# Loading the value windows of a banded attention: own rows of all blocks, and border rows apart

## Chip, core and metric

The kernel runs on one core of one Trainium2 chip. The metric is the device time of one execution in microseconds (us). Three runs of the kernel before took 838.1, 845.5 and 845.78 us; their median is 845.5 us.

## What is computed

An attention with two branches over q, k and v of shape 8 batches x 8 heads x 576 tokens x 64 (float32), and behind it a mixture of 8 experts over the 4608 rows of 512 numbers that the attention gives. The change lies in the local branch of the attention:

```python
pos = np.arange(S)
mask = np.abs(pos[:, None] - pos[None, :]) < 4
scores = np.where(mask, scale * q @ k.T, -1e9)
out_local = softmax(scores) @ v
out_d = softmax(scale * q_d @ k_d.T) @ v_d      # q, k, v averaged over groups of 4 tokens
out = np.repeat(out_d, 4, axis=2) + out_local
# then: each row goes to the expert of its highest score, relu(x @ w1[e]) @ w2[e], times its weight
```

A token sees itself and three neighbours on either side. So a block of 64 queries needs 70 rows of values: its own 64, three above and three below.

## The kernel before, in words

The attention comes first, then the experts. The 8 batches are cut in halves of four heads ("a half": 16 in all), and a half in two units of two heads (32 units). The loop of `attention` is a pipeline written out by hand: in one pass it transposes q and k of unit a (`qk_T`, L344, L345), forms the scores of unit a - 1 (`scores`, L373 and L378: L373 is one matmul in each pass, which marks the pass in the trace), pools k, q and v by four on GpSimd (`pooled`, L358; `pooled_v`, L367), builds a diagonal matrix of maxima on GpSimd (`diagonal`, L405), and for unit a - 2 transposes the weights (`weights_T`, L432), computes the pooled weights (`weights_dT`, L445 and L450: L450 needs that diagonal) and multiplies weights by values (`values_d`, L460; `values`, L478). GpSimd takes its work in order, so the diagonal waits behind the pooling of v. `rows` (L493, L498) transposes results back, `place` picks experts; between passes the first expert's weights are loaded in pieces (`st`, L797), measured (L753, L756, L761) and split.

All loads of the attention go out on SyncE's (SP's) queue, in the order of the program. Twice in a pass pair: `load_v` (L319, the pooled branch's values, tile `ld_v`, one buffer, needed by L367 one pass later), at the end of a pass `load` (L311, eight loads of q and k, 96 partitions x 6 x 64 numbers each) and `load_w` (the value windows, tile `vw`, two buffers, needed by L478 three passes later). Weight pieces and the stores of results (`xd`, L521, L522) go in between.

`vw` holds for one half nine windows of 70 rows for four heads: 70 partitions x 9 windows x 4 heads x 64 numbers. Window g starts at token 64 g - 3; the first window lacks its three upper rows and the last its three lower ones, which are zeroed once at the start. `load_w` fills it with six loads: window 0 from partition 3 on (L326, 67 partitions, four heads), the seven windows in the middle head by head (L329, 70 partitions, four loads), and the last window (L330, 67 partitions, four heads). Every contiguous run is one row of 64 numbers, 256 bytes.

Of the kernel before, what the change touches and what calls it, by code (L numbers as in the profile page):

```python
# [19 lines left out]
B, H, S, D = 8, 8, 576, 64  # L20
# [3 lines left out]
G, QB = S // 64, 32  # L24
WK, WV = QB + 6, 64 + 6
# [23 lines left out]
class Kern:  # L49
# [128 lines left out]
    def attention(self, ctx):  # L178
# [46 lines left out]
        load_v(0)  # L225
        load(1)
        load_w(0)
        load_w(1)
        tail, mid = [], []
        for i in range(-2, n + 1):  # L230
# [58 lines left out]
            if d >= 0 and d % 2 == 1:  # L289
                load_w(d // 2 + 2)  # L290
# [32 lines left out]
    def load_w(self, b, hf, vw):  # L323
        nc = self.nc
        g = self.v[b, 4 * hf:4 * hf + 4]
        nc.sync.dma_start(out=vw[3:, 0], in_=g[:, :WV - 3].rearrange("h p d -> p h d"))  # L326
        for c in range(4):
            mid = bass.AP(g.tensor, g[c, 61:62].offset, [[D, WV], [64 * D, G - 2], [1, D]])
            nc.sync.dma_start(out=vw[:, 1:G - 1, c], in_=mid)  # L329
        nc.sync.dma_start(out=vw[:WV - 3, G - 1], in_=g[:, S - WV + 3:].rearrange("h p d -> p h d"))  # L330

    def bank(self):
        return self.bk.tile([128, 512], F32, name="bank")
# [910 lines left out]
```

## Time and profile before

| | |
|---|---|
| three runs | 838.1, 845.5, 845.78 us |
| the profiled execution | 839.92 us |
| its span, from the first instruction to the last | 838.2 us |
| mean granted TensorE clock | 0.953 |
| busy: PE, DVE, ACT, POOL | 91%, 63%, 50%, 51% of the span |
| attention (first to last matmul of L478) | 24.4 to 342.8 us |

The shares are means over two stages that have different limits, so the stretches of the attention are to be read by themselves. PE is TensorE, PEld its weight loads, DVE is VectorE, ACT ScalarE, POOL GpSimd, SPq the queue on which SyncE issues DMAs. The duration of a row of SPq is the time for which the queue was held by that issue; the transfer goes on behind it. What stands in brackets behind a row is how long its engine sat idle before it and what ended that.

### The profile page before, as it was taken

What the parts mean: (1) busy time and instruction counts of PE and PEld (TensorE: products, weight loads), DVE (VectorE), ACT (ScalarE), POOL (GpSimd) and SP (SyncE); (2) the same over time, 40 slices, a digit from 0 to 9 for tenths busy, and PEclk for the clock granted to TensorE, in tenths of its full rate; (3) what the DMA queues carried; (4) which work ended last, traced back from release to release, by engine and by line L of the source; (5) the groups of instructions that cost most, each with busy time, mean ns of one, the idle gap of its engine ahead of it and who ended that gap; (6) DMA issues with size and microseconds to landing.
All of it is one profiled execution on the core that took longest, in us unless ns stands there. A gap on an engine that the chain in (4) does not pass through costs nothing. (4 is left out here: it accounts for less than half of the span.)

```text
span 838.2 us, 22778 instructions
## 1 busy us (share of the span) xinstructions
PE 761.3 (91%) x8100; PEld 464.3 (55%) x8100; DVE 524.9 (63%) x1501; ACT 417.8 (50%) x807; POOL 430.6 (51%) x815
## 2 busy tenths in 40 slices
PE   7599999999899998969989989899889998998993
PEld 5388778887788887524434444344434444443441
DVE  6358879997769999774653555556373456446430
ACT  3234554444544453326565566667566347546620
POOL 7056564765546667452764445464454535543521
PEclk8769999999889999989998999999999999999997
DMA  8567767576667676583897796969898759858651
GB/s 153 111 140 166 202 131 180 125 206 136 199 134 183 122 176 193 154 205 76 213 193 147 176 222 178 214 140 271 147 218 192 152 116 268 148 132 237 152 97 27
DMA packets 282902, 138.96 MB, mean 166 GB/s; under 512 B 249970, under 2 KB 259186, under 8 KB 282752
## 3 DMA queue, kind: packets, MB, share of 16 engines
q1 hardware_dynamic: 274944, 116.05, 62.0%
q0 software_dynamic: 6560, 19.03, 8.8%
q10 hardware_dynamic: 1248, 2.11, 0.7%
q8 instruction: 66, 1.08, 0.5%
q14 instruction: 84, 0.69, 0.3%
HBM read 213.05 MB, written 20.33 MB: 278 GB/s over the span
## 5 line engine op out<-in xcount | busy, mean ns | idle before, releaser
L1080 PE MATMUL bank<-w1h,xT 128*128 128x512 f16 x328 | 126.3, 385 | 19.1 <-DMA xT<-x 18.6
L1105 PE MATMUL bank<-w2h,hT 128*128 128x512 f16 x328 | 125.0, 381 | 9.8 <-DMA hT<-h 9.8
L1081 PE MATMUL bank<-w1l,xT 128*128 128x512 f16 x328 | 126.1, 384 | 1.6 <-DVEq L925 1.6
L1082 PE MATMUL bank<-w1h,xT 128*128 128x512 f16 x328 | 126.1, 384 | 0.0
L1107 PE MATMUL bank<-w2h,hT 128*128 128x512 f16 x328 | 125.0, 381 | 0.0
L1106 PE MATMUL bank<-w2l,hT 128*128 128x512 f16 x328 | 125.0, 381 | 0.0
L1118 POOL DMA_INDIRECT out_dram<-o,ids x41 | 46.8, 1142 | 134.6 <-ACTq L920 97.1
L1090 DVE SCALAR_TENSOR_TENSOR h<-bank,h 128x512 f16<-128x512 f32 x82 | 55.3, 689 | 93.7 <-ACT h L1089 61.7
L1089 ACT ACTIVATE h<-bank 128x512 f16<-128x512 f32 x82 | 47.7, 595 | 97.1 <-PE bank L1082 57.9
L367 POOL TENSOR_TENSOR pool_v<-ld_v 72x256 f32<-72x256 f32 x64 | 48.6, 770 | 75.7 <-DMA ld_v<-in_v_dram 74.4
L345 ACT ACTIVATE kq<-bank 128x288 f32<-128x288 f32 x128 | 44.1, 416 | 76.3 <-PE bank L344 72.9
L753 ACT ACTIVATE junk<-st 128x1024 bf16<-128x1024 f32 (+1 forms) x30 | 67.5, 2251 | 6.8 <-DVE place L673 5.6
L358 POOL TENSOR_TENSOR pool_kq<-kq 128x288 f32<-128x288 f32 x62 | 43.3, 714 | 48.7 <-ACT kq L345 48.6
L1002 POOL DMA_INDIRECT xg<-xd,ids x41 | 45.5, 1109 | 43.5 <-issue 15.3
L1080 PEld LDWEIGHTS <-xT 128*128 128x128 f16 x328 | 32.5, 99 | 60.9 <-DMA xT<-x 22.1
L1105 PEld LDWEIGHTS <-hT 128*128 128x128 f16 x328 | 34.8, 106 | 45.3 <-DMA hT<-h 10.6
L67 POOL TENSOR_SCALAR nw_t<-nw_y,nw_a 128x1 f32<-128x1 f32 x120 | 52.3, 436 | 12.1
L386 ACT ACTIVATE a<-a 128x342 f32<-128x342 f32 x32 | 15.6, 489 | 83.7 <-DVE a L385 83.7
L1032 DVE SCALAR_TENSOR_TENSOR x<-xg,sc,x 128x512 f16<-128x512 f32 x41 | 30.9, 753 | 42.1 <-ACT x L1029 42.1
L1082 PEld LDWEIGHTS <-xT 128*128 128x128 f16 x328 | 32.5, 99 | 41.7 <-issue 4.1
L1081 PEld LDWEIGHTS <-xT 128*128 128x128 f16 x328 | 32.5, 99 | 39.2 <-issue 2.9
L1107 PEld LDWEIGHTS <-hT 128*128 128x128 f16 x328 | 32.2, 98 | 39.2 <-issue 0.8
(221 smaller groups left out, 1640.6 us busy)
## 6 DMA issues: line engine op xcount, KB each, us to landing
st<-in_moe_w_dram SPq DMA_DIRECT2D x148, 1024.0 KB
ld_k<-in_k_dram SPq DMA_DIRECT2D x64, 144.0 KB
ld_q<-in_q_dram SPq DMA_DIRECT2D x64, 144.0 KB
ld_v<-in_v_dram SPq DMA_DIRECT2D x32, 288.0 KB
xd<-xr SPq DMA_DIRECT2D x8, 1040.0 KB
vw<-in_v_dram SPq DMA_DIRECT2D x64, 122.5 KB
st<-in_moe_w_dram SPq DMA_DIRECT2D x12, 512.0 KB
vw<-in_v_dram SPq DMA_DIRECT2D x32, 67.0 KB
```

Of the source, the lines that this page charges most:

```text
L67: g.tensor_scalar(out=t, in0=y, scalar1=y, scalar2=a, op0=ALU.mult, op1=ALU.mult)
L367: g.tensor_tensor(out=t6[:, c], in0=vr[:, :, 0:2 * D], in1=vr[:, :, 2 * D:], op=ALU.add)
L753: self.nc.scalar.activation(out=junk, in_=src, func=AF.Square, accum_out=acc)
L1080: nc.tensor.matmul(out=ps, lhsT=xT[:, 0, k], rhs=self.w1h[:, k, ns], start=(k == 0), stop=False)
L1081: nc.tensor.matmul(out=ps, lhsT=xT[:, 0, k], rhs=self.w1l[:, k, ns], start=False, stop=False)
L1082: nc.tensor.matmul(out=ps, lhsT=xT[:, 1, k], rhs=self.w1h[:, k, ns], start=False, stop=(k == self.KC - 1))
L1089: nc.scalar.activation(out=h2[:, 0], in_=ps, func=AF.Relu)
L1090: nc.vector.scalar_tensor_tensor(out=h2[:, 1], in0=ps, scalar=0.0, in1=h2[:, 0], op0=ALU.max, op1=ALU.subtract)
L1105: nc.tensor.matmul(out=ps, lhsT=hh, rhs=self.w2h[:, j, :], start=(j == 0), stop=False)
L1106: nc.tensor.matmul(out=ps, lhsT=hh, rhs=self.w2l[:, j, :], start=False, stop=False)
L1107: nc.tensor.matmul(out=ps, lhsT=hl, rhs=self.w2h[:, j, :], start=False, stop=(j == self.FC - 1))
L1118: nc.gpsimd.indirect_dma_start(out=self.out, out_offset=bass.IndirectOffsetOnAxis(ap=self.ids[:, q:q + 1], axis=0), in_=o, in_offset=None, ...
```

## The change

`load_w` alone changes. A half's windows are loaded by ten loads instead of six. Four loads, one for each head, bring the 64 own rows of all nine blocks into partitions 3 to 66. Six loads bring one partition each: partitions 0, 1 and 2 get the row that lies three, two and one tokens above the block, for windows 1 to 8 and four heads; partitions 67, 68 and 69 get the rows below it, for windows 0 to 7. Tiles, buffers, the place in the queue and what is computed stay.

```diff
         g = self.v[b, 4 * hf:4 * hf + 4]
-        nc.sync.dma_start(out=vw[3:, 0], in_=g[:, :WV - 3].rearrange("h p d -> p h d"))
         for c in range(4):
-            mid = bass.AP(g.tensor, g[c, 61:62].offset, [[D, WV], [64 * D, G - 2], [1, D]])
-            nc.sync.dma_start(out=vw[:, 1:G - 1, c], in_=mid)
-        nc.sync.dma_start(out=vw[:WV - 3, G - 1], in_=g[:, S - WV + 3:].rearrange("h p d -> p h d"))
+            own = bass.AP(g.tensor, g[c, 0:1].offset, [[D, 64], [64 * D, G], [1, D]])
+            nc.sync.dma_start(out=vw[3:WV - 3, :, c], in_=own)
+        for p, w0, t0 in [(r, 1, 61 + r) for r in range(3)] + [(WV - 3 + r, 0, 64 + r) for r in range(3)]:
+            edge = bass.AP(g.tensor, g[0, t0:t0 + 1].offset, [[D, 1], [64 * D, G - 1], [S * D, 4], [1, D]])
+            nc.sync.dma_start(out=vw[p:p + 1, w0:w0 + G - 1], in_=edge)
```

## Rows read from the trace of the kernel before

**Rows 1.** Seven stretches, L373 alone: width, PE (count), PEld (count), clock, DMA share, GB/s

```profile
28.60:62.80 34.20, 0.99 (x2) 0.25 (x2) 0.65 0.67 140
62.80:98.80 36.00, 1.24 (x4) 0.39 (x4) 1.00 0.73 191
98.80:111.80 13.00, 0.31 (x1) 0.17 (x2) 0.95 0.53 112
111.80:185.80 74.00, 2.66 (x8) 0.77 (x8) 0.99 0.71 171
185.80:243.50 57.70, 1.91 (x5) 0.60 (x5) 0.85 0.68 158
243.50:317.00 73.50, 2.48 (x8) 0.78 (x8) 1.00 0.68 156
317.00:327.80 10.80, 0.31 (x1) 0.18 (x2) 1.00 0.37 88
```

**Rows 2.** One stretch, all engines: PE, PEld, DVE, ACT, POOL busy, then as above

```profile
243.50:317.00 73.50, 72.61 (x1484) 60.56 (x1482) 67.84 (x173) 36.76 (x94) 45.72 (x63) 1.00 0.68 156
```

**Rows 3.** Timeline of PE: start, duration, line, [idle before and what ended it]

```profile
27.37 0.34 PE L478 MATMUL bank<-aT,vw 70*64 70x64 f32 x4 [1.88 <-DMA vw<-in_v_dram]
...
42.84 0.51 PE L450 MATMUL bank<-dg,onesf 72*72 72x144 f32 x1 [9.22 <-POOL dg L405]
...
195.50 0.34 PE L478 MATMUL bank<-aT,vw 70*64 70x64 f32 x4 [1.88 <-DMA vw<-in_v_dram]
...
222.52 1.57 PE L450 MATMUL bank<-dg,onesf 72*72 72x144 f32 x8 [1.54 <-POOL dg L405]
...
230.99 0.34 PE L761 MATMUL bank<-wsq,onesf 128*128 128x1 f32 x1 [1.00 <-DVE wsq L756]
...
321.96 1.20 PE L450 MATMUL bank<-dg,onesf 72*72 72x144 f32 x8 [1.40 <-POOL dg L405]
```

**Rows 4.** Stretches at the lower granted clock, columns as in Rows 2

```profile
35.60:55.90 20.30, 13.06 (x167) 11.11 (x168) 4.08 (x9) 3.10 (x8) 11.81 (x25) 0.50 0.79 158
196.00:199.40 3.40, 3.40 (x87) 2.89 (x85) 1.50 (x2) 1.64 (x4) 1.31 (x2) 0.51 1.20 213
223.30:236.90 13.60, 12.60 (x168) 10.52 (x167) 5.45 (x14) 5.69 (x12) 8.83 (x14) 0.50 0.50 112
```

**Rows 5.** Timeline of POOL

```profile
39.16 0.72 POOL L367 TENSOR_TENSOR pool_v<-ld_v 72x256 f32<-72x256 f32 x1 [18.44 <-DMA ld_v<-in_v_dram]
```

**Rows 6.** Timeline of SP's queue: start, how long held, line, tile, count

```profile
15.88 0.30 SPq L326 DMA_DIRECT2D vw<-in_v_dram  x1
...
31.40 4.33 SPq L319 DMA_DIRECT2D ld_v<-in_v_dram  x2
...
201.03 0.31 SPq L326 DMA_DIRECT2D vw<-in_v_dram  x1
...
212.32 0.85 SPq L319 DMA_DIRECT2D ld_v<-in_v_dram  x2
...
243.80 0.56 SPq L326 DMA_DIRECT2D vw<-in_v_dram  x1
```

**Rows 7.** The same queue, single issues behind the 67-partition loads L326 and L330

```profile
56.21 3.29 SPq L329 DMA_DIRECT2D vw<-in_v_dram  x1
...
61.63 3.71 SPq L797 DMA_DIRECT2D st<-in_moe_w_dram  x1
```

**Rows 8.** Half a microsecond while L329 is held, and one after; columns as in Rows 2

```profile
58.50:59.00 0.50, 0.50 (x7) 0.50 (x6) 0.47 (x2) 0.48 (x2) 0.00 (x0) 1.00 0.08 18
60.50:61.00 0.50, 0.50 (x18) 0.50 (x16) 0.49 (x2) 0.00 (x0) 0.00 (x0) 1.00 0.77 173
```

**Rows 9.** Views of single lines: engine, operation, count, min/median/max ns

```profile
L326 SPq DMA_DIRECT2D vw<-in_v_dram x16: 268/310/3831, 15.9 to 314.2; - x16
...
L311 SPq DMA_DIRECT2D ld_k<-in_k_dram x64: 318/680/2400, 0.8 to 302.3; - x64
...
L478 PEldq EVENT_SEMAPHORE  x15: 51/51/51, 23.4 to 334.8; - x15
```

## The prediction

> **What bounds the kernel now.** I read the page first (busy shares and the forty slices), then the stretches of the attention by L373, the gaps of PE in its timeline, what each gap waited for, and last SP's queue, which feeds it all.
>
> L373 runs once in a pass, so its count gives the pace [rows 1]. In three stretches the kernel keeps it: 4 passes in 36.0 us, 8 in 74.0 and 8 in 73.5, that is 183.5 / 20 = 9.18 us a pass, at the full granted clock (2.4 GHz). There PE is the bound: 72.61 of 73.5 us busy, with DVE close behind at 67.84 [rows 2]. Elsewhere it loses the pace: 2 passes in 34.2 us, 1 in 13.0, 5 in 57.7, 1 in 10.8. Against 9.18 us these are 15.8, 3.8, 11.8 and 1.6 us too much, 33.0 us together. That is the sum to be had, with the 1.88 us of the first gap ahead of them.
>
> PE's gaps say who is late [rows 3]. At 27.37 and 195.50 PE waits 1.88 us each for `vw` itself. At 42.84 it waits 9.22 us for the diagonal of L405, at 222.52 and 321.96 1.54 and 1.40 us for the same. The diagonal is late because POOL sits ahead of it on L367, waiting for `ld_v`: 18.44 us until 39.16 [rows 5]. At the 13.0 us pass I find no gap that ends in a load of this line; at 230.99 PE waits 1.00 us for DVE's sum of weight squares. These two I do not count as the change's.
>
> Behind each gap the clock falls to its lower level (1.2 GHz, 0.50 or 0.51 in the rows): 35.6 to 55.9, 196.0 to 199.4, 223.3 to 236.9 [rows 4]. Work that PE does there takes twice as long, so half of its busy time is lost: 13.06 / 2 = 6.5, 3.40 / 2 = 1.7 and 12.60 / 2 = 6.3 us. The gaps within the stretches (9.22 + 1.88 + 1.54 + 1.00 + 1.40 = 15.0 us) and the lost clock (14.5 us) make up most of the 33 us; the gaps alone would be half of it.
>
> Why `ld_v` and `vw` are late is in SP's queue. Between 201.03 and 243.80 the queue went through two halves in 42.77 us with one issue right behind the other [rows 6], while two halves are four passes, 36.7 us, at PE's pace. Here the queue, not PE, set the time. And the queue is held by the 67-partition loads. Each brings 67 x 4 = 268 runs of 256 bytes; L326 itself is issued in 0.31 us (median), but the issue behind it is held 3.29 us, and the one behind L330 3.71 us [rows 7, 9]. During such a hold the DMA share is 0.08, about one engine of 16, at 18 GB/s; a little later it is 0.77 and 173 GB/s [rows 8]. 18 GB/s are 70 runs of 256 bytes a microsecond, so 268 runs take 3.8 us: the whole load goes through one engine, and everything behind it stands still.
>
> The Trainium skill ("DMA: Bandwidth & Descriptors", section "Why a DMA increments its semaphore by 16 and not by 1") says a load is spread over the largest number up to 16 that divides the slowest dimension of both sides; 67 is prime, which leaves one engine, and 64 gives 16. The trace agrees with the first half of this by its 0.08 share; no row shows a load of 64 partitions. By its rule a border load (8 blocks) would run on 8 engines and its price would be the issue alone, 6 x 0.27 = 1.6 us instead of the 2.2 us that I take below: 0.6 us less a half.
>
> **The change part by part.** *Removed:* L326, L329 x4, L330. Two such blocks stand between 15.88 and 31.40, 15.5 us [rows 6]; the `ld_v` behind them is held 4.33 us for two issues of which some 0.8 us is its own (the same pair took 0.85 us at 212.32, where nothing held it), so 3.5 us more belong to the last L330. That is 19.0 / 2 = 9.5 us of queue for each half.
>
> *Added, own rows:* four loads of 64 x 9 = 576 runs of 256 bytes. L311's loads are 96 x 6 = 576 runs of 256 bytes too, and take 0.68 us of queue in the median [rows 9]: 4 x 0.68 = 2.7 us. Bounds: its minimum 0.32 (1.3 us) and its maximum 2.40 (9.6 us, no gain; but those are waits behind earlier loads, which I expect to shrink).
>
> *Added, border rows:* six loads of 8 x 4 = 32 runs. From below, the cheapest issue of a 67-partition load, 0.27 us [rows 9]; from above, all 32 runs on one engine at 70 a microsecond, 0.46 us [rows 8]. So 1.6 to 2.8 us; I take the middle, 2.2 us, since neither row is of one partition. Block after: 2.7 + 2.2 = 4.9 us. Saving: 9.5 - 4.9 = 4.6 us of queue a half. The bytes are the same: 4 x 490 + 2 x 268 = 2496 runs before, 4 x 576 + 6 x 32 = 2496 after.
>
> *Added waits:* L478 now depends on up to six border loads and its head's own load. A separate wait instruction on PE's queue takes 51 ns, and there are 15 of them now, one a half [rows 9]. Six more a half would be 16 x 6 x 0.051 = 4.9 us if nothing hid them, none if the queue runs ahead; I take a third, 1.6 us. *Moved:* nothing; the zeroing and the wait for the buffer's last reader stay.
>
> **What follows, stall by stall.** *The first (28.6 to 62.8).* Blocks start at 15.88 as before; two of 4.9 us end at 25.7, `ld_v` goes out by 26.6. Before, its issue ended at 35.73 (31.40 + 4.33) and POOL started at 39.16, 3.4 us later [rows 5, 6]. So POOL starts at 30.0 and PE can start L450 at 33.7 (39.16 to 42.84 is 3.7 us) instead of 42.84: 9.1 us. PE would be there by 42.84 - 9.22 = 33.6, less the 1.88 us of `vw`, so some 2 us of waiting are left and the two gaps are not to be added. The clock still falls; I take the short fall of 3.4 us (1.7 us lost, as after the 1.88 us gap at 195.50) for the long one (6.5): 4.8 us. Together 13.9 us; bounds 9.1 (clock as before) and 15.6 (no fall).
>
> *The second (185.8 to 243.5).* With 2 x 4.6 us off, the queue needs 42.8 - 9.2 = 33.6 us for two halves, under PE's 36.7. Then `vw` and `ld_v` are early, and the 11.8 us go, but for the wait for the weight sum and a short fall of the clock after it (1.0 + 1.7): 9.1 us. Bounds: 1.88 + 1.54 = 3.4 us (gaps alone) and 11.8.
>
> *The last (321.96):* 1.4 us, bounds 0 and 1.6. *The rest* (experts, from 343 us) is only moved forward.
>
> Sum: 13.9 + 9.1 + 1.4 - 1.6 = 22.8 us, from the profiled execution's 839.92 us: 817 us. That execution lies 5.6 us under the median of the three runs (845.5), so against the median the gain could look like 28 us.
>
> **The rivals.** *The clock stays low.* The loads come earlier, but PE still has short idle times, and the clock falls behind them for as long as it does now (1.54 us idle was enough for 13.6 us [rows 3, 4]). Then only gaps go: 9.1 + 3.4 + 1.4 - 1.6 = 12.3 us, 828 us. For it: the fall is not in proportion to the gap. Against: in the 20 passes at the pace the clock is full.
>
> *The holds are not the cause.* At 212.32 `ld_v` was issued without a hold, and still the diagonal was late at 222.52. If `ld_v` is late by its own landing behind weight pieces, an earlier `vw` helps little: 840 us. Against: the weight pieces ahead of that load went out behind an L330, held themselves, in a stretch in which the queue never paused.
>
> *Slower: the border loads hold the queue.* If each was held until the one before it, into the same tile, had landed, 3.4 us as for `ld_v` above, a half's block would be 2.7 + 6 x 3.4 = 23.1 us, 13.6 more than now, and in 16 halves 218 us: some 1058 us. It decides from (9.5 - 2.7) / 6 = 1.13 us per border load on. Against: L329's four issues follow one another without waiting for a landing, though all write one tile.
>
> The Trainium skill ("DMA: Bandwidth & Descriptors", section "Rules for kernel authors") advises against many small transfers: under 64 KB mostly overhead is paid, about 2 us each; these are 8 KB. By that figure, spent in line, a block would be 14.7 us and the kernel some 83 us slower. The rows speak against its use here: the twelve issues of two blocks take 15.5 us with three holds of some 3.5 us among them [rows 6, 7], so about 0.4 us each.
>
> **How the numbers follow.** Forecast (holds gone, most of the clock back) 0.57; clock stays low 0.25; not the cause 0.12; slower 0.06. The first two are gains over 1% (8 us), the third is within it; 1% is about what a measurement of this kernel can tell from no change. So faster 0.82, same 0.12, slower 0.06. The best case of the sum is 839.9 - 33.0 - 1.9 = 805 us. The weak end is the low-clock rival without any hiding of the added waits (839.9 - 9.1 - 3.4 - 1.4 + 4.9 = 831) with the 5.6 us by which the median lies higher: 836 us. The forecast's own range is 808 to 825.
>
> **What would show it.** In the trace after: no issue held over 2 us behind a `vw` load, no half microsecond of the attention at a DMA share of 0.08 for lack of engines; border issues of 0.3 to 0.5 us; the pass of 24 us near 15 or less; L450's waits for L405 under 3 us in all; the clock at its upper level from some 40 us to the end of the attention, but for short falls at the weight sums; the experts' stage as long as before. I am wrong if border issues take over 1.1 us, if POOL still waits many microseconds for `ld_v`, or if the passes lengthen because DVE or ACT now sets them.

## The result, and the profile after

The changed kernel takes 834.81 us (median of 20 runs, 827.56 to 849.93), the kernel before 843.51 us (20 runs). The ratio is 0.987, with a 95% interval of 0.9836 to 0.9903: faster by 1.3%. On another chip it was 0.9929 (0.9883 to 0.9975; run e11 below), 0.7%. The prediction had said 817 us, 22.8 us off the profiled execution; the profiled execution after took 830.29 us, 9.6 us less than the 839.92 us of the one before. The sign was right, and less than half of the gain came.

The passes of the loop are marked by the same matmul, now L374. The stretches below hold the same passes as those of [rows 1]; columns are width, PE (count), PEld (count), clock, DMA share, GB/s. Kernel after:

```profile
27.00:57.00 30.00, 0.80 (x2) 0.25 (x2) 0.77 0.76 142
57.00:93.90 36.90, 1.24 (x4) 0.39 (x4) 1.00 0.74 190
93.90:106.30 12.40, 0.31 (x1) 0.12 (x2) 0.91 0.59 128
106.30:182.50 76.20, 2.66 (x8) 0.81 (x8) 0.97 0.75 168
182.50:233.50 51.00, 1.73 (x5) 0.54 (x5) 0.93 0.80 172
233.50:306.00 72.50, 2.50 (x8) 0.78 (x8) 1.00 0.83 166
306.00:320.00 14.00, 0.31 (x1) 0.25 (x2) 0.72 0.31 100
```

Set against [rows 1], the prediction can be checked stretch by stretch (us; the first line takes in that the first mark came 1.6 us earlier):

| passes | before | after | measured | forecast |
|---|---|---|---|---|
| the first 2 (with the 1.6) | 34.2 | 30.0 | -5.8 | -13.9 |
| the next 4 | 36.0 | 36.9 | +0.9 | 0 |
| the next 1 | 13.0 | 12.4 | -0.6 | 0 |
| the next 8 | 74.0 | 76.2 | +2.2 | 0 |
| the next 5 | 57.7 | 51.0 | -6.7 | -9.1 |
| the next 8 | 73.5 | 72.5 | -1.0 | 0 |
| the last 1 | 10.8 | 14.0 | +3.2 | -1.4 |
| added waits on PE | | | not seen apart | +1.6 |
| sum | | | -7.8 | -22.8 |

The remaining 1.8 us of the 9.6 came behind the last mark.

PE's gaps in its timeline, after:

```profile
37.59 0.76 PE L451 MATMUL bank<-dg,onesf 72*72 72x144 f32 x2 [6.93 <-POOL dg L406]
...
220.97 0.56 PE L762 MATMUL bank<-wsq,onesf 128*128 128x1 f32 x2 [1.96 <-DVE wsq L757]
...
311.84 0.94 PE L599 MATMUL bank<-parts,at 128*128 128x6 bf16 x30 [1.08 <-DVE a L386]
```

Of the gaps of [rows 3] both waits for `vw` are gone, and so are the later waits for the diagonal (1.54 and 1.40 us). The 9.22 us in the first stall have become 6.93 us. The wait for the weight sum has grown from 1.00 to 1.96 us, and a wait for DVE stands in the last pass that was not there before.

Below, a block is what `load_w` issues for one half: in the change four loads of own rows (L328) and six of border rows (L331). `load_v`, `load` and `load_w` are each issued once in a pair of passes, so once a half. What the queue does in the first stall, after (start, how long held, line, tile, count):

```profile
14.52 2.79 SPq L328 DMA_DIRECT2D vw<-in_v_dram  x4
17.35 4.36 SPq L331 DMA_DIRECT2D vw<-in_v_dram  x6
21.83 2.66 SPq L328 DMA_DIRECT2D vw<-in_v_dram  x4
24.53 4.32 SPq L331 DMA_DIRECT2D vw<-in_v_dram  x6
28.95 1.80 SPq L319 DMA_DIRECT2D ld_v<-in_v_dram  x2
```

Two blocks take 14.4 us where the forecast had 9.8 us. The long holds behind `vw` loads [rows 7] are gone. In their place each half has 4.3 us of border issues. The view of the single lines (count, min/median/max ns) says how even that price is:

```profile
L328 SPq DMA_DIRECT2D vw<-in_v_dram x64: 580/634/1641, 14.5 to 300.7; - x64
...
L331 SPq DMA_DIRECT2D vw<-in_v_dram x96: 668/669/1678, 17.4 to 307.0; - x96
...
L479 PEldq EVENT_SEMAPHORE  x61: 51/51/51, 23.9 to 332.8; - x61
```

The own rows cost what the forecast said (4 x 0.63 = 2.5 us against 2.7 us). A border load costs 0.67 us, its minimum equal to its median, where the forecast had 0.37 us and an upper bound of 0.46 us. While they are issued, transfers that went out before are still under way: in the sixteen stretches of border issues the DMA share is 0.37 to 0.84, at 74 to 98 GB/s, as in the first row below, where five of the seven stretches above have 142 to 190 GB/s. Only late in such a stretch can little be left to move, as in the microsecond of the second row. The third and fourth rows are stretches at the lower clock, in the first stall and in the last pass (PE, PEld, DVE, ACT, POOL busy, then clock, DMA share, GB/s):

```profile
24.53:28.85 4.32, 4.32 (x140) 3.79 (x136) 3.07 (x6) 1.32 (x4) 0.00 (x0) 1.00 0.66 95
57.00:58.00 1.00, 1.00 (x69) 0.78 (x67) 0.86 (x4) 0.92 (x4) 0.61 (x1) 1.00 0.04 8
37.59:49.30 11.71, 11.71 (x158) 10.13 (x158) 3.05 (x7) 3.05 (x7) 7.63 (x19) 0.50 0.68 136
312.20:322.40 10.20, 10.20 (x168) 7.80 (x167) 7.90 (x27) 2.48 (x7) 4.63 (x5) 0.50 0.64 220
```

The holds of the kernel before are alike in this: over a whole hold the share is up to 0.59, and in its last part it is 0.08 [rows 8]. The change traded two such holds against six issues that each keep the queue for 0.67 us, longer than the 0.46 us that the prediction had worked out for their data on one engine.

### The profile page after: what moved, and what is told of

The parts are those of the page before. It is cut to its first block, busy times and chain, and to the rows that moved or that the text cites. A ratio compares the mean times of both kernels' runs of the same rounds, so it can differ in the third digit from the quotient of the medians.

```text
span 828.6 us, 22837 instructions
## 1 busy us (share of the span) xinstructions
PE 763.2 (92%) x8100; PEld 464.8 (56%) x8100; DVE 523.7 (63%) x1501; ACT 418.1 (50%) x807; POOL 427.5 (52%) x815
## 3 DMA queue, kind: packets, MB, share of 16 engines
q8 instruction: 66, 1.08, 0.6%
## 5 line engine op out<-in xcount | busy, mean ns | idle before, releaser
L346 ACT ACTIVATE kq<-bank 128x288 f32<-128x288 f32 x128 | 44.0, 416 | 72.9 <-PE bank L345 69.1
L359 POOL TENSOR_TENSOR pool_kq<-kq 128x288 f32<-128x288 f32 x62 | 47.3, 779 | 54.0 <-ACT kq L346 51.2
L368 POOL TENSOR_TENSOR pool_v<-ld_v 72x256 f32<-72x256 f32 x64 | 46.5, 738 | 43.2 <-DMA ld_v<-in_v_dram 41.5
```

The lines of the kernel that those rows point to most:

```text
L359: g.tensor_tensor(out=t2[:, w], in0=k4[:, w, :, 0:2], in1=k4[:, w, :, 2:4], op=ALU.add)
L368: g.tensor_tensor(out=t6[:, c], in0=vr[:, :, 0:2 * D], in1=vr[:, :, 2 * D:], op=ALU.add)
```

## The experiments

Two theories stood after the result. **Theory 1:** the mechanism of the forecast is right, queue time ahead of a late `ld_v`, and the border issues eat the gain. **Theory 2:** the queue has stopped being the bound in the change, and what is left are falls of the clock and other waits. Ratios are to the kernel before, timed on the same chip.

**e1: the change without its border loads.**

```diff
-        for p, w0, t0 in [(r, 1, 61 + r) ...]:          # the six border loads
-            ...
+        if not b:                                        # first two halves: eight loads, as in e2
+            ...
+            return
```

> The change without its border loads: from the second batch on only the four loads of own rows are issued, and the rows above and below the blocks are left out (what stood in the buffers is used); the first two halves are loaded in eight loads, window by window. Theory 1 (the border issues, six of 0.67 us, hold the queue and eat the gain): with a block of 2.7 us of queue instead of 7.2 the gain against the kernel before rises from 9 us to 18 to 24 us, some 820 us. Theory 2 (the queue has stopped being the bound in the change already; what is left are falls of the clock and waits for other work): at most 5 us better than the change, 826 to 834 us.

Measured: 823.17 us, ratio 0.9802 (0.9701 to 0.9903). That is 17 us off the kernel before on this chip, just short of theory 1's 18, and the interval takes in the change's 0.987, so e1 alone doesn't decide between the theories. The first two halves are loaded in another way here, as in e2.

**e2: the kernel before with its two 67-partition loads cut.**

```diff
-        nc.sync.dma_start(out=vw[3:, 0], in_=g[:, :WV - 3]...)
+        nc.sync.dma_start(out=vw[3:WV - 3, 0], in_=g[:, :64]...)
+        nc.sync.dma_start(out=vw[WV - 3:, 0], in_=g[:, 64:67]...)
         for c in range(4): ...                           # 70 partitions, as before
-        nc.sync.dma_start(out=vw[:WV - 3, G - 1], in_=g[:, S - WV + 3:]...)
+        nc.sync.dma_start(out=vw[3:WV - 3, G - 1], in_=g[:, S - 64:]...)
+        nc.sync.dma_start(out=vw[:3, G - 1], in_=g[:, S - 67:S - 64]...)
```

> The kernel before with its two 67-partition loads alone cut into 64 and 3 partitions each; the four loads of 70 partitions stay; eight loads a half. Theory 1: no hold of 3.3 to 3.7 us is left and the block costs 8 issues of 0.3 to 0.5 us, 3 to 4 us of queue; 818 to 826 us, better than the change. Theory 2: as good as the change and no better, 830 to 837 us. If the holds were not the cause at all: 840 to 845 us, as before.

Measured: 827.45 us, 0.9834 (0.9693 to 0.9974), an interval too wide to settle it; e10 below repeats it. Its trace is the clearest of all. SP's queue, the second half's block and the `ld_v` behind it:

```profile
20.18 0.59 SPq L326 DMA_DIRECT2D vw<-in_v_dram  x1
20.81 0.47 SPq L327 DMA_DIRECT2D vw<-in_v_dram  x1
21.33 1.84 SPq L330 DMA_DIRECT2D vw<-in_v_dram  x4
23.27 0.59 SPq L331 DMA_DIRECT2D vw<-in_v_dram  x1
23.90 0.47 SPq L332 DMA_DIRECT2D vw<-in_v_dram  x1
24.47 0.77 SPq L319 DMA_DIRECT2D ld_v<-in_v_dram  x2
```

No issue is held: the block takes 4.3 us, and `ld_v` leaves at 24.47 instead of 31.40. PE's wait in the first stall, and then the stretch of the first two passes, in the columns of L374's table above:

```profile
32.01 0.34 PE L452 MATMUL bank<-dg,onesf 72*72 72x144 f32 x1 [0.86 <-POOL dg L407]
```

```profile
27.60:46.10 18.50, 0.62 (x2) 0.20 (x3) 1.00 0.84 165
```

The first stall is all but gone (0.86 us), the clock stays up, and two passes take 18.5 us: 9.25 us each, PE's pace. That is what the prediction had drawn, at the 4.9 us a block that it had assumed (PE at L450 at 33.7; here 32.0). All 29 passes together take 281.4 us, against 293.0 in the change: 11.6 us less, of which 11.5 us are in these two passes (18.5 against 30.0). So the change lacks the first stall above all; what it lacks in the later passes is taken up at e10. The profiled execution of e2 took 831.95 us all the same, more than the 830.29 us of the change: behind the last mark it took 521.1 us, the change 508.5 us. Over the thirteen profiled executions of this document this rest is 504 to 521 us, and no run shows why; so single executions are compared here by their passes and not by their whole times.

**e3: what an issue costs.** Five small loads of different shapes, each on a line of its own, in place of the border loads.

```diff
+        nc.sync.dma_start(out=vw[0:1, 1:9], in_=row(8, 4, 61))     # L340: 1 partition, 32 runs
+        nc.sync.dma_start(out=vw[1:2, 1:5], in_=row(4, 4, 62))     # L341: 1 partition, 16 runs
+        nc.sync.dma_start(out=vw[2:3, 1:2], in_=row(1, 4, 63))     # L342: 1 partition, 4 runs
+        nc.sync.dma_start(out=vw[67:68, :8, 0], in_=one)           # L344: 1 partition, 8 runs
+        nc.sync.dma_start(out=vw[67:70, :8, 1], in_=three)         # L346: 3 partitions, 24 runs
```

> A measurement of issues: after the four loads of own rows, five loads, each on a line of its own: one partition x 8 windows x 4 heads (32 runs of 256 bytes), one partition x 4 windows x 4 heads (16 runs), one partition x 4 heads (4 runs), one partition x 8 windows (8 runs), three partitions x 8 windows (24 runs). The other border rows are left out from the second batch on. If the issue of a border load is paid by the run (21 ns each by 0.67 us / 32), the five take 0.67, 0.34, 0.1 to 0.3, 0.2 to 0.3 and 0.5 us. If it is paid by having one partition, the first four all take 0.67 us and the fifth 0.3 us. If it is a price of any small load, all take 0.67 us.

Measured, in the views of the five lines (count, min/median/max ns):

```profile
L340 SPq DMA_DIRECT2D vw<-in_v_dram x14: 722/731/2087, 49.8 to 287.7; - x14
...
L341 SPq DMA_DIRECT2D vw<-in_v_dram x14: 667/678/690, 50.6 to 289.8; - x14
...
L342 SPq DMA_DIRECT2D vw<-in_v_dram x14: 587/593/594, 51.4 to 290.5; - x14
...
L344 SPq DMA_DIRECT2D vw<-in_v_dram x14: 632/635/809, 52.0 to 291.2; - x14
...
L346 SPq DMA_DIRECT2D vw<-in_v_dram x14: 438/446/453, 52.7 to 292.0; - x14
```

With one partition 4, 8, 16 and 32 runs cost 0.59, 0.64, 0.68 and 0.73 us: from 4 to 32 runs only 0.14 us more, some 5 ns a run. Part of that is the place: L340 comes right behind a load of own rows, and in the change, too, the border load at that place takes 0.73 us (median of sixteen) and the last four of a block 0.67 us. So the price is not paid by the run, and a border load is dear at any length. Three partitions with 24 runs cost 0.45 us, less than one partition with 4. Why, these rows don't say. Of the three expectations, a price of having one partition came nearest.

**e4: the border rows in eight loads of three partitions, one head each.**

```diff
+        for c in range(4):
+            for p, w0, t0 in ((0, 1, 61), (WV - 3, 0, 64)):
+                edge = bass.AP(g.tensor, g[c, t0:t0 + 1].offset, [[D, 3], [64 * D, G - 1], [1, D]])
+                nc.sync.dma_start(out=vw[p:p + 3, w0:w0 + G - 1, c], in_=edge)
```

> The change with its border rows in eight loads of three partitions x 8 windows, one head each, instead of six loads of one partition. By theory 1 it is better than the change if such an issue takes under 0.5 us (8 x 0.4 = 3.2 us against 4.3 us of queue a half): 1 to 4 us better. By theory 2 no difference, 830 to 837 us.

Measured: 824.39 us in its one run, some 10 us under the change's median, which was taken on another chip; one run can't carry more than "not worse". The issue is cheaper than in e3, though the shape is that of L346: the first of the eight, behind a load of own rows, takes 0.50 us, the others 0.24 to 0.28 us in the median. The first stall is as long as in the change all the same:

```profile
L332 SPq DMA_DIRECT2D vw<-in_v_dram x128: 241/276/1486, 18.1 to 299.7; - x128
```

```profile
35.65 0.52 PE L452 MATMUL bank<-dg,onesf 72*72 72x144 f32 x1 [6.83 <-POOL dg L407]
```

```profile
25.20:56.40 31.20, 0.80 (x2) 0.27 (x3) 0.73 0.77 146
56.40:313.70 257.30, 8.37 (x27) 2.77 (x28) 0.99 0.77 168
```

Its two first blocks and the gaps between them still take 12.8 us ahead of `ld_v` (15.26 to 28.05), 1.6 us less than in the change, and PE still waits 6.83 us. What this execution gained in the attention lies in the 27 passes behind: 257.3 us, where the change has 263.0 us; but there two executions of one kernel can differ by 4.6 us (e2 and e10, below).

**e5: the change, with the second half's windows behind the first `load_v` of the loop.**

```diff
         load_w(0)
-        load_w(1)
...
                 if a % 2:
                     load_v(a // 2 + 1)
+                    if a == 1:
+                        load_w(1)
```

> The change, with the second half's windows loaded behind the first load_v of the loop instead of ahead of it; nothing else moves. Theory 1 (the queue is held by border issues, and what it costs falls in the first stall above all, where two blocks of 7.2 us stand ahead of one late ld_v): ld_v goes out 7 us earlier, PE's wait of 6.93 us for the diagonal goes, the pass of 20.5 us falls to 10 to 12 us; some 8 us better than the change, 822 to 828 us. Theory 2 (falls of the clock and other waits set the time): the pass stays over 15 us and the time within 3 us of the change.

Measured: 826.17 us, 0.9773 (0.9714 to 0.9832), about 8 us better than the change. The queue and PE in the profiled execution (which took 834.46 us, the longest of the four):

```profile
22.77 0.86 SPq L320 DMA_DIRECT2D ld_v<-in_v_dram  x2
...
39.01 0.28 PE L346 MATMUL bank<-ident,ld_q 96*128 96x96 f32 x1 [1.65 <-DMA ld_q<-in_q_dram]
```

`ld_v` leaves at 22.77 instead of 28.95, and of the wait for the diagonal in this stall 0.17 us are left. PE now waits 1.65 us for q, which comes behind the moved windows. The first two passes take 22.2 us instead of 30.0 us; the pass of 20.5 us has become one of 11.9 us. Nothing of the change was altered but its place in the queue at one point, and most of what it lacked came back. Theory 2 falls for the first stall.

**e6: the same move in the kernel before.** The diff is that of e5.

> The kernel before, with the same move and with its six loads as they were. Theory 1: the first stall falls (ld_v is 9.7 us earlier), but the holds of 3.3 to 3.7 us stay in every later half: 5 to 13 us better than before, and passes of 11 to 16 us stay about the 15th to the 20th. If the holds cost nothing outside the first stall, it would be as good as the change with the move (822 to 828 us).

Measured: 836.12 us, 0.9946 (0.9904 to 0.9988): 4.5 us by the ratio, just under the lowest of what theory 1 expected. The holds stay, and PE still waits in the later stretch for `vw` and for the diagonal:

```profile
190.27 0.34 PE L479 MATMUL bank<-aT,vw 70*64 70x64 f32 x4 [2.34 <-DMA vw<-in_v_dram]
...
217.03 0.34 PE L451 MATMUL bank<-dg,onesf 72*72 72x144 f32 x1 [1.61 <-POOL dg L406]
```

Both waits are gone in the change. e5 against e6 gives what the change is worth with the move in both: 0.9773 against 0.9946, 1.7%. It isn't worth that in the later halves alone: in the profiled executions the first two passes take 22.2 us in e5 and 25.7 us in e6, the 27 behind them 264.0 and 268.9 us.

**e7: the border loads from ScalarE's queue.**

```diff
-            nc.sync.dma_start(out=vw[p:p + 1, w0:w0 + G - 1], in_=edge)
+            nc.scalar.dma_start(out=vw[p:p + 1, w0:w0 + G - 1], in_=edge)
```

> The change, with its six border loads issued from ScalarE's queue instead of SyncE's. Theory 1 (it is the time of the issue on SyncE's queue that counts): SyncE's block falls to 2.7 us, the first pass to 15 us or less; 820 to 828 us, unless ScalarE, which then spends 4.3 us a half on issues, holds PE up. If the transfers of one partition themselves slow the DMA engines, it is no better than the change, 832 to 838 us.

Measured: 1019.4 us, ratio 1.2115 (1.2036 to 1.2194). Theory 1 had allowed for ScalarE's time on issues, not for this. The issues cost the same there, 0.676 us, but they also wait before they go out, and ScalarE's arithmetic, which comes behind them in order, waits with them. The view of the line, the largest sum of waits on ScalarE up to 500 us (us in total, times, longest), and the first of them in the timeline:

```profile
L331 ACTq DMA_DIRECT2D vw<-in_v_dram x96: 675/676/793, 4.0 to 473.8; - x96
```

```profile
ACT kq L346 <- DMA vw<-in_v_dram: 124.4, 9, 21.4
```

```profile
6.22 19.84 ACTq L331 DMA_DIRECT2D vw<-in_v_dram  x11
26.11 2.53 ACT L346 ACTIVATE kq<-bank 128x288 f32<-128x288 f32 x8 [21.39 <-DMA vw<-in_v_dram]
```

ScalarE's copies of q and k (L346) stood 124.4 us behind the line of the border loads, and with them PE. Eleven issues of 0.676 us are 7.4 us; these took 19.84 us, and in these first two halves no reader of the buffer comes ahead of them. What they wait for there is not shown. The experiment says nothing on what it was made for, whether transfers of one partition slow the DMA engines; e8 and e2 together do, below.

**e8: six more small loads a half.**

```diff
             nc.sync.dma_start(out=vw[p:p + 1, w0:w0 + G - 1], in_=edge)
+            few = bass.AP(g.tensor, g[0, t0:t0 + 1].offset, [[D, 1], [64 * D, 1], [S * D, 4], [1, D]])
+            nc.sync.dma_start(out=self.spare[p:p + 1], in_=few)
```

> The change with six more one-partition loads of 4 runs each a half, into a tile that nobody reads, each behind a border load. By the issue price of such a load (0.59 us) a block grows from 7.2 to some 11 us of queue, over the 9.5 us of the kernel before. Theory 1: the gain is lost, 842 to 856 us, with ld_v late again in the first stall (PE waits over 9 us there) and in later halves. Theory 2: no more than 3 us slower than the change.

Measured: 868.88 us, 1.0319 (1.0255 to 1.0383), worse than theory 1 had said. The block starts at 14.98 and the next at 26.05, 11.1 us as expected; PE waits for the diagonal in the first stall and, 3.10 us, in a later half again:

```profile
14.98 2.79 SPq L329 DMA_DIRECT2D vw<-in_v_dram  x4
...
26.05 2.66 SPq L329 DMA_DIRECT2D vw<-in_v_dram  x4
...
37.13 0.86 SPq L320 DMA_DIRECT2D ld_v<-in_v_dram  x2
```

```profile
44.80 0.51 PE L454 MATMUL bank<-dg,onesf 72*72 72x144 f32 x1 [10.59 <-POOL dg L409]
...
241.20 0.52 PE L454 MATMUL bank<-dg,onesf 72*72 72x144 f32 x1 [3.10 <-POOL dg L409]
```

The added loads carry 1 KB each, and the issues follow one another without a wait, so it is next to nothing but issue time that costs some 34 us against the change's median. Whether transfers of one partition slow the load behind them can be told from the same rows: from the end of `ld_v`'s issue to PE's start of the line that waits for it are 6.81 us here, behind 24 loads of one partition (37.99 to 44.80), 6.84 us in the change behind 12 (30.75 to 37.59), and 6.77 us in e2 behind none (25.24 to 32.01). They don't.

**e9, e10, e11: the cut loads with and without the move, and the change, on one chip.** e9 has the diffs of e2 and e5, e10 that of e2, e11 is the change.

> The 67-partition loads cut into 64 and 3 (eight loads a half, 4.4 us of queue), and the second half's windows loaded behind the first load_v of the loop. Theory 1 (queue time ahead of ld_v): with blocks of 4.4 us the first stall is nearly gone already, so the move adds 0 to 3 us; 820 to 826 us, ratio to before 0.972 to 0.982. If the move helps as much here as with the change (8 us), the length of the block was not what made the first stall.

> The cut loads alone, once more and in more rounds, beside the change on the same chip: 821 to 828 us, ratio to before 0.975 to 0.985, and 5 to 10 us better than the change. If it is within 3 us of the change, the issue price of the border loads is not what the change lacks.

> The change itself on the same chip: ratio to before 0.983 to 0.991 as before, and a pass of 15 us or more in the first stall again.

| kernel | median us | ratio | 95% interval |
|---|---|---|---|
| e9, cut and moved | 820.92 | 0.976 | 0.9705 to 0.9814 |
| e10, cut | 821.1 | 0.978 | 0.9729 to 0.9831 |
| e11, the change | 838.95 | 0.9929 | 0.9883 to 0.9975 |

The first two passes and the 27 behind them, in e10 and then in e11 (columns as for L374):

```profile
27.20:45.70 18.50, 0.62 (x2) 0.22 (x3) 1.00 0.86 163
45.70:304.00 258.30, 8.37 (x27) 2.77 (x28) 0.98 0.73 172
```

```profile
26.20:57.90 31.70, 0.80 (x2) 0.27 (x3) 0.73 0.73 139
57.90:323.20 265.30, 8.57 (x27) 2.79 (x28) 0.97 0.75 164
```

The cut loads beat the change with intervals that don't meet, by 18 us in the median, more than the 5 to 10 us expected; e11's 0.9929 lies above the 0.983 to 0.991 expected of it. The move adds nothing that can be told apart to the cut loads, while it gave the change 8 us. So the length of the blocks ahead of the first `ld_v` is what the first stall hangs on: 13.2 us of difference in the first two passes. Behind them e10 is 7.0 us ahead of e11, but two executions of the same kernel, e2 (262.9 us) and e10 (258.3 us), already differ by 4.6 us there, so what the border issues cost in the later passes is not settled. Nor is the first stall's length in one execution a matter of the blocks alone: e1 has e2's loads in its first two halves, but PE got there earlier, waited 3.07 us, and took 25.3 us for the two passes. Cutting two loads is also the smaller edit: it beats both kernels.

By queue time of a block these kernels come in order: 4.3 us (e2, e10) 0.978 to 0.983; 7.2 us (the change) 0.987 to 0.993; 9.5 us (before) 1; 11.1 us (e8) 1.032. e1, with 2.7 us from the third half on, adds nothing to that (0.980).

## Why the prediction was right and wrong

**Right: what held the queue.** The issue behind a 67-partition load was held for 3.2 to 4.1 us in 29 of 32 cases, and in the last part of the hold the transfers went at the pace of about one engine. With no such load no issue of the window loads is held for 2 us (L328's worst is 1.64 us, L331's 1.68 us), though loads of q and k still are at times (3.75 us at worst, 3.84 us before). The kernel of e2, which does nothing but cut the two loads, is 2.2% faster than the kernel before on e10's chip. The rival "the holds are not the cause" falls.

**Right: the chain to PE.** The forecast's way from the issue of `ld_v` to PE (3.4 us to POOL, 3.7 us to L450) holds: after, the issue ends at 30.75 (28.95 + 1.80), and 30.75 + 3.4 + 3.7 = 37.85; measured 37.59. Where a block took even less than the forecast's 4.9 us (4.3 us, e10), 0.978 came out, some 18 us of the 22.8 us.

**Wrong: the step "Added, border rows".** It took 0.37 us an issue, between 0.27 us (a 67-partition load's cheapest issue) and 0.46 us (32 runs through one engine). It is 0.67 us: 4.3 us a half instead of 2.2 us. Both bounds were prices of other shapes: the lower of a load with 67 partitions, the upper of moving data, while e3 shows a price that barely depends on the runs and is higher for one partition than for three. The saving of queue was 9.5 - 7.2 = 2.3 us a half instead of 4.6 us. In the first stall, where two blocks stand ahead of one `ld_v`, that is 4.6 us lost; `ld_v` itself was held 1.80 instead of 0.85 us; and the blocks started 1.4 us earlier (14.52 instead of 15.88), which was luck: nothing in the forecast says it. So PE started the line that needs the diagonal 5.3 us earlier (42.84 to 37.59) instead of 9.1 us. Two of the prediction's own signs of being right failed with it: the long pass was to be near 15 us and is 20.5 us, and the waits for the diagonal were to be under 3 us and are 6.93 us.

**Wrong: the clock of the first stall.** The forecast let the long fall shrink to 3.4 us. PE worked for 11.71 us at the lower level behind its wait (37.59 to 49.30, the row above), so 5.9 us of work time was lost there instead of 1.7 us; before it was 6.5 us. The 5.3 us of earlier start and these 0.6 us are the 5.8 us of the table, where the forecast had 9.1 + 4.8. The price of the border loads has its part in this too, since it left 6.93 us of waiting in place of some 2 us. But the term was unsafe in itself: behind 2.54 us of waiting at this place the clock stayed at 1.00 (e3), behind 3.07 us it was 0.50 for 10.2 us (e1), and with 0.86 us (e2) it stayed at 1.00.

**Nearly right: the second stall.** 6.7 us against 9.1 us. The waits for `vw` and `ld_v` went as forecast; the wait for the weight sum, put at 1.0 us and a short fall, is 1.96 us, with a mean clock of 0.93 over 51.0 us, 7.1 us at the lower level.

**Wrong: the last pass.** 1.4 us less was forecast, 3.2 us more came. The wait for the diagonal went, but right behind it PE meets L599, which waits for DVE, and the clock falls for 10.2 us: 5.1 us lost for a gap of 1.08 us (some 3.9 us of it ahead of the last mark). Before, L598 was ready when PE got there, because PE had waited 1.40 us just ahead of it [rows 3]. The wait that was taken away had covered the next one: the forecast had this term as a plain gain, with no look at what came behind. In the thirteen profiled executions a wait of 1.08 to 1.94 us at this line stands in the eight whose last pass took 13.9 to 15.4 us, and in none of the other five, with 10.2 to 10.8 us. No experiment took it away alone, so that the fall of the clock comes from it is well supported but not shown. Nor is it shown why the eight passes from 106.3 on took 2.2 us longer; their mean clock is 0.97 against 0.99.

**The added waits on PE.** There are 61 now instead of 15 [rows 9], 46 more, 2.3 us if nothing hid them; the forecast had 1.6 us. No stretch shows them apart.

**The rivals.** "The clock stays low" (828 us) came closest, and in the first stall the clock did give little back. That its number is so near the 830.29 us is partly luck: it, too, had 9.1 us for the first wait, where 5.3 us came, had only 3.4 us for the second stall, where 6.7 us came, and did not have the loss in the last pass. Slower by border loads was wrong in kind, since they follow one another without a wait; their 0.67 us lies between the forecast's 0.37 us and the break-even of 1.13 us. e8 has crossed that break-even: 6 x 0.67 + 6 x 0.59 = 7.6 us of small issues a half, more than the 6.8 us that the prediction allowed.

## What to carry to other kernels

Count a queue's time in issues, not in bytes: look for the issue that is held, and read from the line before it what holds it. When a load with an awkward number of partitions is split, price the pieces from an issue of the very shape, or measure one, before many small pieces replace two large loads; here cutting 67 into 64 and 3 was worth 2.2%, and reordering all the windows 0.7 to 1.3%. And of a wait that is taken away ask which late neighbour it was covering.

## What the runs showed of the hardware

The issue of a load into one partition costs 0.59 us with 4 runs of 256 bytes (e3, e8) and 0.67 us with 32, 0.73 us right behind a larger load (the change); into three partitions 0.45 us behind a load of one (e3), 0.24 to 0.28 us behind another of three and 0.50 us behind one of 64 (e4). It is the same from ScalarE's queue (0.676 us, e7) as from SyncE's (0.669 us). On ScalarE, though, a load that has to wait stops the arithmetic behind it: 1019 us.

Behind a load of 67 partitions the next issue on the queue was held for 3.2 to 4.1 us in 29 of 32 cases. The other DMA engines first work off what went out before (a DMA share of up to 0.59 over a whole hold); in the half microsecond near its end the share was 0.08, at 18 GB/s, in 31 of the 32. The same rows as 64 and 3 partitions cost 0.59 and 0.47 us of queue (e2).
